# A fused attention, gelu-layer and expert kernel: its hand-written order made anew, with the second weight matrix narrowed in PSUM

## The chip, the cores and the metric

The kernel runs on one core of one Trainium2 chip. The metric is the device time of one launch in microseconds, and the time before is the median of three runs. The engines are TensorE (PE in the views, its weight loads PEld), VectorE (DVE), ScalarE (ACT), GpSimd (POOL) and SyncE (SP), which only issues transfers here. L931 is line 931 of the kernel.

## The reference

Three layers follow each other. First comes attention over 4 batches of 576 positions with 8 heads of 64, in which a position sees itself and the 63 before it; then a feed-forward layer with the gelu form h * sigmoid(1.702 h); then a layer of 8 experts of which each token takes its best two.

```python
scores = np.where(mask, (q @ k.T) / 8, -1e9)      # mask: 0 <= row - column < 64
x = softmax(scores) @ v                            # 2304 tokens x 512
h = x @ w_in                                       # 512 x 2048, float64
x = (h * (1.0 / (1.0 + np.exp(-1.702 * h)))) @ w_out   # 2048 x 512, float64
noisy = x @ w_gate + np.log1p(np.exp(x @ w_noise)) * noise
top2, top2_w = best_two(noisy)                     # weights: softmax of the two
out[t] = sum over the two of top2_w * (np.maximum(x[t] @ w1[e], 0.0) @ w2[e])
```

## The kernel before, in words

The 2304 tokens make 18 tiles of 128. A tile holds 128 rows of one batch; tiles 8 and 17 hold the last 64 rows of two batches each. Three tiles make a chunk (c = 0 to 5). A chunk's attention leaves xT, its first layer turns that into 16 products (f = 0 to 15) and its second layer sums these up into three output tiles. Every operand of a matmul is held as two float16 halves (a high part and the rest, "lo"), and a product is three matmuls (high by high, high by low, low by high). After the six chunks come the eight experts, in which rows are gathered by slot and the results are added into the output.

**The order written out.** For chunks 0 and 1, and the attention of tiles 0 to 9, every engine's order is the text SEQ, a list of some 760 short names; the loop behind `manual = tc.manual_schedule` emits them one after the other, and each engine works through its own in that order. A name's first part is a function (the table `ops`), its numbers are a tile, a piece or an f. The ones that matter here:

- `lk`, `lq`, `lv`: loads of a tile's k, q, v (lines 126 to 160), issued by SyncE. `wl`: load of one of 32 pieces of the two gelu-layer matrices (line 202), SyncE too.
- `na`, `nb`, `nc`: three VectorE steps (lines 214, 220, 226) that narrow a piece from float64, read as pairs of 32-bit words, to float32. Pieces 0 to 15 are of the first matrix, 16 to 31 of the second. `ch`, `cs`, `cl`: high half and scaling (ScalarE), low half (GpSimd, line 256).
- Tiles below NPE: `pt_` transposes q or k on TensorE (line 524), `ph_` and `pl_` take the halves out of PSUM (ScalarE 533, VectorE 537), `tp`, `th`, `tl` the same for the probabilities (600, 604, 607), and the scores are made by line 514. Other tiles: `qh` (ScalarE 401), `ql` (GpSimd 410), `kt` (SyncE 417), `q2` (two VectorE copies, 421 and 422), `qt` (SyncE 427), and for the probabilities `ph`, `pl`, `pt` (580, 583, 588), with the scores of line 488. `sh`, `sl`, `st` make tile 2's k once more in the second form for tile 3.
- `sc`, `mm`, `ex`, `rc`, `nm`, `pv`: scores, mask and maximum, exponentials, reciprocal, normalising, probability times V. `vh`, `vl`: halves of v. `e1`, `e2`: high and low half of xT (ScalarE 632, VectorE 638).
- `s1.f`, `t1.f`: the 12 matmuls of the first layer's product f of chunk 0 and 1 (line 667), into PSUM buffers "h" (two), for some f of chunk 0 "y" (two). `gt`, `gm`, `gh`, `gl` (and `ut` to `ul` for chunk 1): tanh (672), gelu product (675), high and low half (678, 681).
- `s2.f`, `z2`: second layer of chunk 0 and 1 (line 702). `yh`, `yl`: output halves (707, 710). `x2`, `lo`: SyncE transposes an output tile (739), TensorE makes its logits (750 to 753). `ra` to `ri`: routing.
- `cn`, `cg`, `cz`, `fd`: transfers of the noise (8), the gate weights (2), a zero row (1) and the slot table's fill (1), issued by SyncE (lines 345, 350, 355, 356, 339, 382).

**Behind the order.** The rest is placed by slots, one per 12 or so matmuls: the list `slots` holds the matmul steps from chunk 2 on, and before each slot all `tasks` that are due by it are emitted (`at`). Tile 10's loads and preparation are due between the slots 52 and 57 and so come right behind the order, tile 11's eight slots later. The steps of the routing of chunk c are due at fixed slots behind the chunk: `route_g` (three rank matmuls, line 825, that wait for r_M of line 814) at 12.

The buffers that the change touches are drawn from pools by tag: "r" (one PSUM bank), "h" (two PSUM banks), "wf" (two SBUF buffers of float32), "wst" (three SBUF buffers for loaded pieces). A new use of a tag waits until the use that many places earlier has been read.

Of the kernel before, what the change touches and what calls it, by code (L numbers as in the profile page):

```python
# [37 lines left out]
NPE = 3  # L38
# [7 lines left out]
pl_.2.1 wl.5 lv.2 rc.1.0 st.2 nc.3 cl.2 vl.1 na.4 tp.0.1 sc.2.0 lq.3 th.0.1 nm.1.0 mm.1.1 wl.6 lk.5 tp.1.0 tl.0.1 ch.3
nb.4 nc.4 cs.3 fc sc.2.1 va.1 ex.1.1 wl.7 th.1.0 na.5 rc.1.1 mm.2.0 nm.1.1 ch.4 vh.2 nb.5 tp.1.1 qh.3 mm.2.1 cl.3 nc.5
cs.4 pv.0.1 ql.3 ex.2.0 ex.2.1 wl.16 cl.4 na.6 nb.6 e1.0 rc.2.0 vl.2 nc.6 q2.3 ch.5 kt.3 ch.6 cs.5 wl.8 cl.5 e2.0
th.1.1 lq.5 tl.1.0 tl.1.1 va.2 cs.6 na.7 nb.7 cl.6 rc.2.1 nm.2.1 nm.2.0 pv.1.0 pv.1.1 qh.5 nc.7 na.16 nb.16 ch.7 na.8
nc.16 qt.3 tp.2.0 nb.8 e1.1 cs.7 e2.1 cl.7 th.2.0 tl.2.0 nc.8 tp.2.1 ch.16 cs.16 wl.9 th.2.1 lv.3 ch.8 sc.3.1 tl.2.1  # L50
pv.2.0 pv.2.1 sc.3.0 lk.4 na.9 cs.8 mm.3.1 e1.2 cl.8 wl.10 lq.4 e2.2 wl.11 nb.9 ex.3.1 cl.16 nc.9 s1.4 rc.3.1 s1.2
lv.4 ql.5 ch.9 na.10 s1.1 cs.9 nb.10 wl.18 gt.4 qh.4 nm.3.1 nc.10 ch.10 cl.9 cs.10 gm.4 gt.2 na.11 cl.10 nb.11 nc.11
gh.4 mm.3.0 s1.0 gt.1 ch.11 ql.4 vh.3 gm.2 cs.11 gh.2 gm.1 wl.12 gh.1 ex.3.0 s1.10 cl.11 ph.3.1 na.18 fd nb.18 gt.10
q2.4 kt.4 nc.18 gm.10 s1.7 ch.18 gh.10 na.12 gl.4 gt.0 s1.5 gl.2 wl.17 cs.18 rc.3.0 qt.4 s1.11 gm.0 nb.12 gt.5 na.17
wl.13 q2.5 pl.3.1 cl.18 pt.3.1 gm.5 gl.1 nc.12 nb.17 gt.11 gl.10 sc.4.0 gh.5 gm.11 nm.3.0 s1.8 s1.9 ch.12 nc.17 gt.7
# [24 lines left out]
e2.9 ri.0 yh.3 yl.3  # L80
# [17 lines left out]
def fused_kernel(ctx, tc, q, k, v, w_in, w_out, w_gate, w_noise, noise, w1, w2, out, cap=CAP):  # L98
# [186 lines left out]
    def consts_a():  # L285
# [11 lines left out]
        for t in range(3):  # L297
            dve.tensor_copy(m[0:64, t, 0:64], le[0:64])
            dve.tensor_copy(m[0:64, t, 64:128], gt[0:64])
            dve.tensor_copy(m[64:128, t, 0:64], (le if t == 2 else gt)[64:128])  # L300
            dve.tensor_copy(m[64:128, t, 64:128], (gt if t == 2 else le)[64:128])
# [169 lines left out]
    def scores(i, g):  # L471
# [562 lines left out]
    for c in range(NCH):  # L1034
# [7 lines left out]
        for fn, dt, dl in ((route_a, 5, 3.1), (route_b, 6, 3.2), (route_c, 7, 3.3), (route_d, 8, 3.4), (route_e, 10, 3.5),  # L1042
                           (route_f, 11, 3.6), (route_g, 12, 5), (route_h, 12, 5.2), (route_i, 13, 5.1)):
# [135 lines left out]
```

## Time and profile before

| what | us |
|---|---|
| three runs | 953.22, 956.4, 961.06 |
| median | 956.4 |
| the profiled execution | 955.65 |
| its span, first to last instruction | 954.0 |

The profile is one execution. Its rows give busy time, mean time of one instruction and the idle time of the engine just before a group, with what ended it ("releaser"). A row of the timeline gives start, length, engine, line, operation, and in brackets an idle time before it and its releaser. PEclk is the clock granted to TensorE as a share of full speed.

### The profile page before, as it was taken

What the parts mean: (1) busy time and instruction counts of PE and PEld (TensorE: products, weight loads), DVE (VectorE), ACT (ScalarE), POOL (GpSimd) and SP (SyncE); (2) the same over time, 40 slices, a digit from 0 to 9 for tenths busy, and PEclk for the clock granted to TensorE, in tenths of its full rate; (3) what the DMA queues carried; (4) which work ended last, traced back from release to release, by engine and by line L of the source; (5) the groups of instructions that cost most, each with busy time, mean ns of one, the idle gap of its engine ahead of it and who ended that gap; (6) DMA issues with size and microseconds to landing.
All of it is one profiled execution on the core that took longest, in us unless ns stands there. A gap on an engine that the chain in (4) does not pass through costs nothing. (4 is left out here: it accounts for less than half of the span.)

```text
span 954.0 us, 16355 instructions
## 1 busy us (share of the span) xinstructions
PE 883.7 (93%) x6315; PEld 504.0 (53%) x6315; DVE 501.3 (53%) x1020; ACT 388.5 (41%) x884; POOL 381.2 (40%) x372
## 2 busy tenths in 40 slices
PE   6597899997889999989999999998999999999994
PEld 4464445544545544644544556655564747465561
DVE  7999998762662662681372732354252525243220
ACT  5677576632552752751551421243140405141110
POOL 3467768523571561561361432341314132322111
PEclk9999999998899999999999999999999999999997
DMA  9999689936778737812137992798594949493212
GB/s 224 204 221 238 139 228 168 186 70 126 203 196 147 129 61 142 175 27 67 45 114 169 183 195 38 170 264 194 110 223 75 239 77 244 90 216 74 32 20 39
DMA packets 264948, 137.47 MB, mean 144 GB/s; under 512 B 217120, under 2 KB 241504, under 8 KB 264864
## 3 DMA queue, kind: packets, MB, share of 16 engines
q1 hardware_dynamic: 228640, 76.55, 41.3%
q0 software_dynamic: 11680, 27.30, 13.7%
q10 hardware_dynamic: 24544, 32.51, 11.8%
q8 instruction: 51, 0.84, 0.4%
q14 instruction: 33, 0.27, 0.1%
HBM read 76.46 MB, written 21.07 MB: 102 GB/s over the span
## 5 line engine op out<-in xcount | busy, mean ns | idle before, releaser
L931 PE MATMUL o<-w,gb 128*128 128x512 f16 x960 | 209.9, 379 | 0.6 <-DVE gb L914 0.6
L702 PE MATMUL y<-w,gb 128*128 128x512 f16 x816 | 186.8, 382 | 4.8 <-DVE gf L675 3.3
L924 PEld LDWEIGHTS <-w 128*128 128x128 f16 x1536 | 150.1, 98 | 63.2 <-issue 2.7
L667 PEld LDWEIGHTS <-w 128*128 128x128 f16 x1152 | 112.3, 100 | 95.9 <-issue 25.4
L954 POOL DMA_INDIRECT out_dram<-ot,me x40 | 70.3, 1758 | 231.3 <-DVE ot L951 227.2
L931 PEld LDWEIGHTS <-gb 128*128 128x128 f16 x960 | 93.6, 98 | 111.4 <-DVE gb L914 1.5
L667 PE MATMUL h<-xT,w 128*128 128x384 f16 x744 | 138.0, 339 | 14.6 <-DVE gf L675 12.0
L702 PEld LDWEIGHTS <-gb 128*128 128x128 f16 x864 | 82.6, 98 | 101.8 <-issue 9.2
L924 PE MATMUL h<-xe,w 128*128 128x384 f16 (+1 forms) x840 | 126.5, 302 | 2.4 <-DVE gb L914 2.4
L681 POOL TENSOR_TENSOR gb<-gf,gb 128x384 f16<-128x384 f32 x96 | 95.8, 1004 | 81.1 <-ACT gb L678 78.6
L951 DVE TENSOR_SCALAR ot<-o,me 128x512 f32<-128x512 f32 x40 | 30.0, 751 | 140.4 <-PE o L931 122.6
L267 DVE SCALAR_TENSOR_TENSOR w<-wst,w 128x1024 f16<-128x1024 f32 x64 | 79.4, 1241 | 45.5 <-ACT w L248 45.5
L924 PE MATMUL y<-xe,w 128*128 128x256 f16 (+1 forms) x696 | 102.1, 297 | 0.0
L913 ACT ACTIVATE gb<-y 128x256 f16<-128x256 f32 (+1 forms) x58 | 24.9, 430 | 179.5 <-PE y L924 179.4
L248 ACT ACTIVATE w<-wst 128x1024 f16<-128x1024 f32 x64 | 67.5, 1056 | 39.3 <-DVE w L267 14.2
L908 POOL DMA_INDIRECT xg<-x2buf,me x40 | 43.2, 1080 | 81.3 <-DMA me<-xmeta 40.3
L667 PE MATMUL y<-xT,w 128*128 128x384 f16 x408 | 71.5, 330 | 0.9 <-DVE gf L675 0.9
L678 ACT ACTIVATE gb<-gf 128x384 f16<-128x384 f32 x96 | 49.3, 516 | 40.6 <-DVE gf L675 39.8
L562 ACT ACTIVATE sm<-sm,st 128x128 f32<-128x128 f32 x144 | 55.9, 390 | 12.0 <-DVE st L556 11.9
L410 POOL TENSOR_TENSOR qk<-kq,qk 128x1024 f16<-128x1024 f32 x15 | 32.9, 2195 | 68.7 <-ACT qk L401 67.5
L913 ACT ACTIVATE gb<-h 128x384 f16<-128x384 f32 (+1 forms) x70 | 30.7, 439 | 63.3 <-PE h L924 62.3
L914 DVE SCALAR_TENSOR_TENSOR gb<-h,gb 128x384 f16<-128x384 f32 (+1 forms) x70 | 34.6, 494 | 40.1 <-ACT gb L913 40.1
(163 smaller groups left out, 962.7 us busy)
## 6 DMA issues: line engine op xcount, KB each, us to landing
wst<-in_moe_w_dram ACTq DMA_DIRECT2D x62, 512.0 KB, 4.4
wst<-in_moe_w_in_dram SPq DMA_DIRECT2D x16, 512.0 KB, 5.0
wst<-in_moe_w_out_dram SPq DMA_DIRECT2D x16, 512.0 KB, 4.0
x2buf<-R SPq DMA_DIRECT2D x18, 256.0 KB, 3.1
kq<-in_k_dram SPq DMA_DIRECT2D x16, 256.0 KB, 5.5
kq<-in_q_dram SPq DMA_DIRECT2D x16, 256.0 KB, 4.2
vv<-in_v_dram SPq DMA_DIRECT2D x16, 256.0 KB, 4.7
out_dram<-z POOLq DMA_DIRECT2D x3, 1280.0 KB, 5.8
```

The source lines that it names most:

```text
L248: act.activation(o[:, 0], i, AF.Copy, scale=s)
L267: dve.scalar_tensor_tensor(o[:, 1], i, s, o[:, 0], op0=ALU.mult, op1=ALU.subtract)
L562: act.activation(sm[:, u, :], sm[:, u, :], AF.Exp, bias=st[:, 0, u:u + 1], accum_out=st[:, 1, u:u + 1])
L667: pe.matmul(hp, w[:, a, d, fs], xt[:, x + d, :], start=n == 0, stop=n == 11)
L678: act.activation(g1[:, f, 0], GF[c, f], AF.Copy)
L681: pool.tensor_tensor(g1[:, f, 1], GF.pop((c, f)), g1[:, f, 0], op=ALU.subtract)
L702: pe.matmul(YP[i], g1[:, f, a, 128 * j:128 * j + 128], w[:, s, f % 8, :], start=f == 0 and a + s == 0, stop=f == 15 and a == 1)
L908: pool.indirect_dma_start(out=xg, out_offset=None, in_=src, in_offset=bass.IndirectOffsetOnAxis(ap=ME[e, part][:, t, 9:10], axis=0))
L913: act.activation(o[:, 0], hp, AF.Relu)
L924: pe.matmul(hp, w[:, a, d, 128 * f:128 * f + 128], x[:, s + d, :], start=m == 0, stop=m == 11)
L931: pe.matmul(yp, lhs[:, f, a, :], w[:, s, f, :], start=f == 0 and a + s == 0, stop=f == 7 and a == 1)
L954: s = pool.indirect_dma_start(out=out, out_offset=bass.IndirectOffsetOnAxis(ap=ids, axis=0), in_=ot, in_offset=None, compute_op=ALU.add)
```

## The change

What it does, in six parts:

- SEQ is written anew: the same operations in another sequence, apart from tile 3, which is handled as tiles 0 to 2 are (NPE 3 to 4), and tile 10, whose loads and preparation (`lk`, `lq`, `lv`, `qh`, `ql`, `kt`, `q2`, `qt`, `vh`, `vl`, `va`) now stand in the list.
- The second matrix's pieces: the first two narrowing steps write to a PSUM buffer of the tag "h" and the third reads it and writes to "wf", as the first matrix's pieces do with "r".
- `cn`, `cg`, `cz`, `fd` (12 transfers) are issued by GpSimd.
- Tiles 8 and 17 load v in two transfers of 128 rows instead of four of 64, with the older 64 rows in partitions 0 to 63; the mask and the score columns of these tiles are swapped to match.
- `route_g`, `route_h`, `route_i` and the scatters of chunks 1 to 4 are due one slot later.
- Behind the list nothing else differs; tasks that the list has done are left out.

```diff
-NPE = 3
+NPE = 4
...
 SEQ = """
-lk.0 cid lq.0 pt_.0.0 wl.0 lk.1 ph_.0.0 pt_.0.1 lq.1 ca pl_.0.0 ph_.0.1 fa pl_.0.1 na.0 sc.0.0 pt_.1.0 ph_.1.0 sc.0.1
...
+cid lk.0 wl.0 lq.0 pt_.0.0 fa pt_.0.1 ca na.0 ph_.0.0 ph_.0.1 nb.0 pl_.0.0 nc.0 pl_.0.1 ch.0 wl.2 sc.0.0 na.2 nb.2
...
+z2.2.0 nm.8.0 pt.7.1 ul.14 yl.2 lv.9 sc.9.0 cn ex.8.1
+ph.8.0 pv.7.0 rc.8.1 lo.0 pv.7.1 e1.7 um.10 uh.12 nm.8.1 uh.10 pl.8.0 t1.13 vh.9 vl.9 ul.12 x2.1 ut.13 x2.2 z2.1.1
+ph.8.1 mm.9.0 pl.8.1 mm.9.1 vl.8 e2.7 ex.9.0 ex.9.1 ul.10 ci t1.15 pt.8.0 um.13 uh.13 ql.10 lo.1 z2.2.1 rc.9.0 pv.8.0
...
 """
...
-        sp.dma_start(vv[0:64], rows(v, b, 512, 64))
-        sp.dma_start(vv[64:128], rows(v, b, 448, 64))
-        sp.dma_start(vb[0:64], rows(v, b + 1, 512, 64))
-        sp.dma_start(vb[64:128], rows(v, b + 1, 448, 64))
+        sp.dma_start(vv, rows(v, b, 448, 128))
+        sp.dma_start(vb, rows(v, b + 1, 448, 128))
...
-            o = NW[key, p] = T(pm, [128, 512], F32, "r", 1) if key[0] == "in" else T(mp, [128, 512], F32, "wf", 2)
+            o = NW[key, p] = T(pm, [128, 512], F32, *(("r", 1) if key[0] == "in" else ("h", 2)))
...
-            o = T(mp, [128, 512], F32, "wf", 2) if key[0] == "in" else i
+            o = T(mp, [128, 512], F32, "wf", 2)
...
-        sp.dma_start(x2buf[0], C["z"])
+        pool.dma_start(x2buf[0], C["z"])
...
-            sp.dma_start(nz[:, i0:i0 + 4], noise[b * S:b * S + 512].rearrange("(t p) e -> p t e", p=128))
+            pool.dma_start(nz[:, i0:i0 + 4], noise[b * S:b * S + 512].rearrange("(t p) e -> p t e", p=128))
...
-                       (route_f, 11, 3.6), (route_g, 12, 5), (route_h, 12, 5.2), (route_i, 13, 5.1)):
+                       (route_f, 11, 3.6), (route_g, 13, 5), (route_h, 13, 5.2), (route_i, 14, 5.1)):
```

Counted in the two lists, VectorE's operations up to and with `e2.5` (tile 5's low half of xT, for which the first matmul of `t1` waits):

| operation | old | new |
|---|---|---|
| narrowed pieces of the first matrix | 16 | 16 |
| narrowed pieces of the second matrix | 8 | 10 |
| `pl_` and `tl` (low halves taken out of PSUM) | 12 | 16 |
| `q2` (swaps) | 4 | 3 |
| `mm`, `rc`, `gm`, `vl`, `e2` | 13, 12, 16, 6, 6 | 13, 12, 16, 6, 6 |

And TensorE's from the first `t1` to the end of the list, in both: 16 `t1`, 9 `s2`, 12 `z2`, 6 `sc`, 8 `pv`, 3 `lo`. Between the first `s1` and the first `t1` the new list has two `tp` more. Ahead of the first `s1` it has two `pt_` more and otherwise the same counts.

## Rows read from the trace of the kernel before

**Rows 1.** Timeline of TensorE: first s1, first t1, end of the written order.

```profile
53.84 3.02 PE L667 MATMUL h<-xT,w 128*128 128x384 f16 x12
...
122.57 5.85 PE L667 MATMUL h<-xT,w 128*128 128x384 f16 x35 [0.45 <-DVE xT L638]
...
219.34 4.06 PE L667 MATMUL h<-xT,w 128*128 128x384 f16 x24
```

**Rows 2.** Busy time by stretch: length, engines (x instructions), clock, transfer share, GB/s.

```profile
0.00:53.80 53.80, 35.36 (x384) 27.49 (x384) 46.93 (x99) 34.62 (x93) 21.64 (x26) 1.00 0.96 220
53.80:121.80 68.00, 57.20 (x494) 31.55 (x488) 64.67 (x93) 46.33 (x120) 52.05 (x44) 0.95 0.86 200
121.80:185.20 63.40, 57.65 (x497) 32.34 (x496) 53.62 (x82) 40.02 (x109) 44.01 (x56) 0.97 0.96 189
185.20:219.30 34.10, 34.10 (x250) 16.08 (x244) 21.46 (x75) 14.71 (x38) 8.11 (x7) 1.00 0.39 77
219.30:280.00 60.70, 50.52 (x401) 28.09 (x400) 33.18 (x90) 29.86 (x77) 37.00 (x36) 0.89 0.77 193
```

**Rows 3.** TensorE's waits, 53.8 to 219.4: total us, times, longest.

```profile
PE h L667 <- DVE gf L675: 3.6, 3, 2.2
PE x L623 <- DVE xT L638: 3.4, 1, 3.4
```

**Rows 4.** VectorE's groups by shape, 0 to 219: busy us, mean ns, idle before.

```profile
L226 DVE SCALAR_TENSOR_TENSOR wf<-wst,wf 128x512 int32<-128x512 int32 x16 | 18.7, 1167 | 0.2
L220 DVE SCALAR_TENSOR_TENSOR wf<-wst,wf 128x512 int32<-128x512 int32 x16 | 16.1, 1006 | 0.2
L214 DVE TENSOR_SCALAR wf<-wst 128x512 int32<-128x512 int32 x16 | 14.7, 921 | 3.0 <-POOL w L256 3.0
...
L220 DVE SCALAR_TENSOR_TENSOR r<-wst,r 128x512 int32<-128x512 int32 x16 | 11.0, 689 | 0.2
L214 DVE TENSOR_SCALAR r<-wst 128x512 int32<-128x512 int32 x16 | 11.0, 686 | 0.1
L226 DVE SCALAR_TENSOR_TENSOR wf<-wst,r 128x512 int32<-128x512 int32 x16 | 10.9, 680 | 0.8
...
L421 DVE COPY qk<-qk 128x512 f16<-128x512 f16 x7 | 8.5, 1219 | 0.0
...
L422 DVE COPY qk<-qk 128x512 f16<-128x512 f16 x7 | 4.6, 658 | 0.0
```

**Rows 5.** Timeline of TensorE: scores in both forms, one group of transposes.

```profile
21.28 2.38 PE L514 MATMUL s<-kT,qT 64*128 64x64 f16 x36
...
28.38 1.11 PE L600 MATMUL y<-idn,sm 128*128 128x128 f32 x4
...
147.15 0.77 PE L488 MATMUL s<-kT,qT 128*128 128x64 f16 x24
```

**Rows 6.** Timelines behind the order: SyncE, ScalarE, GpSimd, VectorE, TensorE.

```profile
222.83 0.43 SPq L128 DMA_DIRECT2D kq<-in_k_dram  x1
...
227.71 1.06 ACT L401 ACTIVATE qk<-kq 128x1024 f16<-128x1024 f32 x1 [7.57 <-DMA kq<-in_q_dram]
...
228.84 2.12 POOL L410 TENSOR_TENSOR qk<-kq,qk 128x1024 f16<-128x1024 f32 x1 [29.14 <-ACT qk L401]
...
231.00 0.29 DVE L421 COPY qk<-qk 128x512 f16<-128x512 f16 x1 [10.13 <-POOL qk L410]
...
229.52 0.19 PE L753 MATMUL r<-wr,x2T 128*128 128x32 f16 x1 [1.21 <-DMA x2T<-R]
...
232.01 3.22 PE L667 MATMUL h<-xT,w 128*128 128x384 f16 x13 [2.12 <-DVE gf L675]
...
236.38 0.24 PE L488 MATMUL s<-kT,qT 128*128 128x64 f16 x1 [1.15 <-DMA qT<-qk]
```

**Rows 7.** TensorE's waits, 219 to 500: total us, times, longest.

```profile
PE r L825 <- DVE r_M L814: 3.3, 2, 2.6
```

**Rows 8.** GpSimd's own transfer issues (ns min/median/max), and a VectorE copy beside them.

```profile
L202 POOL DMA_DIRECT2D wst<-in_moe_w_dram x2: 826/899/972, 165.1 to 168.9; - x2
...
165.43 3.73 DVE L421 COPY qk<-qk 128x512 f16<-128x512 f16 x1
```

More of the change, by code (lines that the diff above doesn't have):

```diff
@@ L46 @@
[L46 to L55, printed above, removed]
@@ new lines @@
+pv.1.0 pt_.3.0 vh.2 ex.2.0 fd lk.4 na.6 vh.3 mm.2.1 th.1.1 ch.5 wl.7 tl.1.1 rc.2.0 pt_.3.1 ph_.3.0 cl.4 na.17 ex.2.1
+nm.2.0 nb.6 pl_.3.0 pv.1.1 vl.2 ph_.3.1 e1.1 lq.4 va.2 tp.2.0 rc.2.1 pl_.3.1 nc.6 cs.5 nm.2.1 tp.2.1 th.2.0 ch.6 cs.6
+cl.5 nb.17 th.2.1 tl.2.0 na.7 nc.17 lk.5 tl.2.1 qh.4 cl.6 e2.1 ch.17 wl.8 sc.3.1 nb.7 pv.2.0 pv.2.1 vl.3 nc.7 cs.17
+ql.4 e1.2 mm.3.1 na.8 lq.5 e2.2 nb.8 wl.16 sc.3.0 wl.9 qh.5 q2.4 s1.1 lk.6 cl.17 ch.7 nc.8 na.16 ex.3.1 kt.4 rc.3.1
+cs.7 ch.8 ql.5 s1.2 wl.10 cs.8 na.9 qt.4 cl.7 cl.8 nb.16 nb.9 nc.9 gt.2 nc.16 gt.1 ch.9 gm.1 ch.16 mm.3.0 wl.11 gm.2
@@ new lines @@
+cs.16 s1.6 cs.9 gt.6 s1.0 gh.1 nm.3.1 na.10 lq.6 gt.0 wl.12 cl.9 nb.10 tp.3.1 s1.9 gl.1 gh.2 gm.0 ex.3.0 gm.6 nc.10
+th.3.1 gl.2 cl.16 q2.5 wl.13 gt.9 rc.3.0 na.11 va.3 gm.9 nb.11 gh.0 gl.0 ch.10 s1.5 sc.4.0 cs.10 gt.5 nc.11 gm.5 ch.11
+sc.4.1 nm.3.0 gh.6 cs.11 cl.11 tp.3.0 tl.3.1 s1.8 gh.9 na.12 qh.6 mm.4.0 s1.3 mm.4.1 nb.12 cl.10 ex.4.0 qt.5 nc.12
+gl.6 th.3.0 ql.6 na.13 gt.8 gt.3 wl.18 ch.12 gm.3 tl.3.0 s1.4 gl.9 gh.5 s1.10 cs.12 gm.8 pv.3.0 gh.3 rc.4.0 nb.13
+wl.14 nc.13 gl.5 na.18 nm.4.0 cl.12 ex.4.1 gh.8 gl.8 s1.7 gl.3 rc.4.1 gt.10 kt.5 ch.13 na.14 wl.20 nb.18 nm.4.1 kt.6
@@ new lines @@
+gm.10 lv.4 nc.18 gt.4 gt.7 cs.13 gm.4 q2.6 wl.15 sc.5.0 ph.4.0 ch.18 gm.7 ph.4.1 qt.6 cl.13 s1.11 gh.10 na.20 pl.4.0
+nb.14 nb.20 cs.18 pl.4.1 gh.7 nc.14 ch.14 mm.5.0 pv.3.1 cs.14 cl.18 ex.5.0 nc.20 sc.5.1 wl.19 cl.14 gt.11 ch.20 na.15
+s1.12 nb.15 wl.24 nc.15 gh.4 s1.14 ch.15 gm.11 s2.0 vh.4 gl.10 gl.4 e1.3 s2.1 gt.12 rc.5.0 sc.6.1 gh.11 nm.5.0 gt.14
+cs.20 lv.5 mm.5.1 pt.4.0 gm.12 wl.22 vl.4 cs.15 na.19 ex.5.1 nb.19 cl.20 vh.5 nc.19 gh.12 gl.7 ch.19 sc.6.0 cs.19
+gm.14 rc.5.1 e2.3 cl.15 na.24 ph.5.0 nb.24 nc.24 s1.15 gt.15 gh.14 s2.2 wl.21 ch.24 pt.4.1 pv.4.0 gm.15 vl.5 na.22
@@ new lines @@
+cl.19 na.21 cs.24 nb.22 gl.11 nc.22 pl.5.0 wl.28 nm.5.1 s2.3 nb.21 ch.22 cl.24 ph.5.1 va.5 pv.4.1 cs.22 pl.5.1 e1.4
+pt.5.0 nc.21 mm.6.1 ch.21 cl.22 s1.13 na.28 s2.4 e2.4 pv.5.0 wl.23 cs.21 gh.15 gt.13 cl.21 nb.28 s2.5 gm.13 gh.13
+nc.28 gl.14 na.23 nb.23 ch.28 cs.28 pt.5.1 pv.5.1 e1.5 ex.6.1 nc.23 gl.15 cl.28 wl.25 e2.5 ch.23 na.25 nb.25 nc.25
+cs.23 s2.6 t1.0 wl.26 lk.7 rc.6.1 gl.12 ut.0 um.0 t1.2 cl.23 lq.7 lv.6 ut.2 mm.6.0 uh.0 ex.6.0 t1.3 um.2 lk.9 ut.3
+lq.9 wl.27 na.26 um.3 nb.26 nc.26 gl.13 nm.6.1 s2.7 qh.7 ch.25 ch.26 ph.6.1 ql.7 pl.6.1 ul.0 cs.26 t1.4 t1.6 s2.8 vh.6
@@ L81 @@
+pt.8.1 z2.2.2 nm.9.0 ul.13 ph.9.0 ut.15 z2.1.2 rc.9.1 um.15 kt.10 uh.15 nm.9.1 pl.9.0 pv.8.1 lv.10 ph.9.1 ul.15 z2.1.3
+lo.2 z2.2.3 yh.4 pl.9.1 ra.0 cu rb.0 pt.9.1 yl.4 rq.0 pt.9.0 e1.8 rd.0 e2.8 vh.10 z2.0.0 re.0 yh.5 q2.10 qt.10 pv.9.0
+rf.0 z2.0.1 pv.9.1 z2.0.2 e1.9 rh.0 e2.9 rg.0 vl.10 z2.0.3 yh.3 va.10 yl.5 ri.0 yl.3
 """
@@ L297, in consts_a @@
         for t in range(3):
[L298 to L301, printed above, removed]
+            dve.tensor_copy(m[0:64, t, 0:64], (gt if t == 2 else le)[0:64])
+            dve.tensor_copy(m[0:64, t, 64:128], (le if t == 2 else gt)[0:64])
+            dve.tensor_copy(m[64:128, t, 0:64], gt[64:128])
+            dve.tensor_copy(m[64:128, t, 64:128], le[64:128])
         dve.memset(m[0:64, 1, 64:128], MASK)
@@ L349, in consts_n @@
                     r0 = (b + j) * S + 512
-                    sp.dma_start(nz[64 * j:64 * j + 64, i], noise[r0:r0 + 64])
+                    pool.dma_start(nz[64 * j:64 * j + 64, i], noise[r0:r0 + 64])
         C["nz"] = nz
@@ L354, in consts_g @@
         wg = T(cst, [128, 4, 2 * E], F32, "wg")
-        sp.dma_start(wg[:, :, 0:E], w_gate.rearrange("(c p) e -> p c e", p=128))
-        sp.dma_start(wg[:, :, E:], w_noise.rearrange("(c p) e -> p c e", p=128))
+        pool.dma_start(wg[:, :, 0:E], w_gate.rearrange("(c p) e -> p c e", p=128))
+        pool.dma_start(wg[:, :, E:], w_noise.rearrange("(c p) e -> p c e", p=128))
         C["wg"] = wg
@@ L481, in scores @@
             parts = [[(64 * j, 64 * j + 64, c0, c0 + 64, kk, 64 * j) for j in range(2)]
-                     for c0, kk in ((0, k1), (64, KT[i]))]
+                     for c0, kk in ((0, KT[i]), (64, k1))]
         for pp in parts:
@@ L1048, in fused_kernel @@
             for a in range(2):
-                at(t0 + (5.4 if last else (14 if c else 17 + P["r0"]) + 2 * j + a), scatter, c, j, a)
+                at(t0 + (5.4 if last else (15 if c else 17 + P["r0"]) + 2 * j + a), scatter, c, j, a)
     for n in range(4):
```

43 lines of the change are left out of this document (14 added, 29 removed).

## The prediction, made before the changed kernel ran

> **What bounds the kernel now.** I read the stretches first, because the change is confined to the order written out by hand and the few steps behind it. The order ends where TensorE starts on the third chunk, at 219.34 us [rows 1]. Up to 121.8 us the limit is VectorE: it works 46.93 of the first 53.80 us and 64.67 of the next 68.00, while TensorE stands still for 18.44 and 10.80 us [rows 2]. From 121.8 to 185.2 us VectorE still works 53.62 of 63.40, TensorE idles 5.75, and from 185.2 us to the end of the order TensorE never stops. Then, from 219.3 to 280 us, TensorE loses 10.18 us again, with a granted clock of 0.89 [rows 2]. In the view of TensorE's waits the two largest after the first first-layer matmul are on VectorE: 3.6 us on the gelu product (gf) and 3.4 on the low half of xT [rows 3]. So work taken from VectorE moves TensorE up to about 185 us; work given to TensorE costs nothing only while it idles.
>
> **VectorE, the narrowing of the second matrix.** The three narrowing steps of one piece take 0.921 + 1.006 + 1.167 = 3.094 us with the intermediate in SBUF (second matrix) and 0.686 + 0.689 + 0.680 = 2.055 with it in PSUM (first matrix), over 16 pieces each [rows 4]. The edit gives the second matrix the PSUM form: 16 x 1.04 = 16.6 us less VectorE work. That the same integer steps would not get faster in PSUM is excluded by these rows.
>
> **Part A, up to the first matmul of chunk 1's first layer.** At 122.57 us this matmul waited for tile 5's xT low half on VectorE [rows 1], so VectorE's work ahead of that step sets it. By the counts listed with the change, both orders have the same masks, maxima, gelu products and v splits ahead of it. The old one has 8 pieces of the second matrix, the new one 10; the new one has 4 more low-half subtractions (tile 3 on TensorE) and one q swap less. So 10 x 2.055 - 8 x 3.094 = -4.2 us; the four subtractions read PSUM as the narrowing's last step does, at about 0.68 us [rows 4], +2.7; the swap's two copies, 1.219 + 0.658 [rows 4], -1.9. Sum -3.4 us: the first t1 comes at about 119.2 us. VectorE also idles 53.80 - 46.93 + 68.00 - 64.67 = 10.2 us there; the new order may shrink or stretch this. I take no change; the ends are a gain of 10.2 and, as nothing excludes it, a loss as large.
>
> **Tile 3 on TensorE.** Two score groups of 36 matmuls (2.38 us) take the place of 24 (0.77), and four groups of transposes at 1.11 us are added [rows 5]: 3.2 + 4.4 us. The probability-times-V groups keep 24 matmuls each, in the slower form, which by the scores' ratio (2.38/36 against 0.77/24) doubles each of them; estimate 0.8 each, 1.6 us. Together 9.3 us, all before the first t1, where TensorE idles 29.2 us: cost 0. Only two transposes and the two V groups (3.8 us) stand behind the first first-layer matmul, where 10.80 us idle remain as cover; uncovered they would cost 3.8. GpSimd, ScalarE and the transposing transfers lose work by it; I count nothing for that.
>
> **Part B, from the first t1 to the end of the order.** Both orders hold the same TensorE work there (the counts agree), and it took 219.34 - 122.57 = 96.8 us. Losses in it: 5.75 us idle, and a clock of 0.97 over 63.4 us [rows 2], which as a mix of its two levels, 2.4 and 1.2 GHz, is 3.8 us at half speed, 1.9 us lost: 7.65 in all. VectorE has 6 pieces of 2.055 left where it had 8 of 3.094, 12.3 instead of 24.8 us; tile 10 brings back one swap (1.9) and one v split, whose price no row here has (no more than another 2). It falls from 53.6 to about 45 of 63 us. The waits on VectorE should go; waits on a transfer stay, and the borrowed PSUM buffers (below) can make new ones. I take 5 of the 7.65; the ends are 7.65 and the cost of the second rival. Then the order ends at 119.2 + 91.8 = 211.0 instead of 219.3: 8.4 us gained by A and B.
>
> **Part C, tile 10's loads.** At present SyncE issues them only at 222.83, behind the transpose of the last output rows. From there runs one chain: ScalarE waits 7.57 us for the q load and begins at 227.71, GpSimd begins its difference at 228.84, VectorE's copy stands 10.13 us at the head of its queue until 231.00, and the gelu product of the new chunk, queued behind, makes TensorE wait 2.12 us; the scores wait 1.15 for qT, and the second logits transpose, which SyncE issues behind these loads, makes it wait 1.21 [rows 6]. All of it is moved into the order: 4.5 us of stalls. What is late next is tile 11, whose preparation is not moved. Ends: all 10.18 us idle and the lost half of the clock, (1 - 0.89) x 2 x 60.7 / 2 = 6.7 [rows 2], against 0 if tile 11 stalls in its place. I take 4.5.
>
> **Part D, the rank matmuls one slot later.** TensorE waited for r_M in two places, 3.3 us in all [rows 7]. A slot is some 2 us of matmuls, so most of it is hidden; I take 1.5, between 0 and 3.3, and a loss of the same size if the later rank step delays the scatters behind it.
>
> **Issues.** Twelve transfers go from SyncE to GpSimd: the fill of the slot table, the zero row, eight for the noise, two for the gate weights. One issue holds GpSimd for 0.826 to 0.972 us [rows 8], so 12 x 0.9 = 10.8 us, of which the eight for the noise, 7.2, come in one piece. Queued behind those are low halves of g1 that TensorE reads only after 24 first-layer and 24 second-layer matmuls; at the 5.85 us that 35 first-layer ones took [rows 1] that is 8 us or more of cover. I take 0; uncovered it costs 7.2. SyncE loses these and two loads at tile 8; nothing waits there now that I price. On the sign of their conflict with VectorE the row says that VectorE loses: a copy, 1.219 us on average [rows 4], lasted 3.73 while GpSimd worked and issued [rows 8]. The Trainium skill, "SBUF - State Buffer", section "SBUF: two separate sides", says that a transfer issued from GpSimd is starved while VectorE runs an operation in a two-port mode, with 3.1 us in place of 0.62; by that, twelve would cost GpSimd some 37 us (an estimate from that page), and no row here shows an issue so long.
>
> **Sum.** 8.4 + 4.5 + 1.5 = 14.4 us. The profiled execution took 955.65 us (span 954.0); 955.65 - 14.4 = 941.25. It lies 0.75 under the median of the runs, so I predict 942 us.
>
> **Rivals.**
> 1. *VectorE's time turns into waiting.* In a fixed order each step also waits for ScalarE, GpSimd and the transfers. Then A and B give nothing, tile 3's 3.8 us are uncovered, C and D stay: 955.65 + 0.75 + 3.8 - 6 = 954.2 us. For it: the transfer engines are 0.86 to 0.96 busy up to 185 us [rows 2]. Against: the largest waits name VectorE. Chance 0.28.
> 2. *The borrowed buffers, slower than before.* The second matrix's intermediate now takes one of the two "h" buffers in which first-layer results land. Each of 16 pieces leaves TensorE a single one until its third step is through. A wait for such a buffer shows now as h <- gf, 1.2 us on average, 2.2 at most [rows 3]. Sixteen at 1.2 add 19 us: 961; at 2.2, 35 us: 977. It decides from 12 waits at the mean or 7 at the longest, where the 14.4 are eaten. Against: VectorE runs ahead of TensorE in the new order and the three steps last 2.1 us. Chance 0.14.
> 3. *Starved issues.* If each noise issue lasts as long as that copy, 8 x 3.73 = 30 us stand in front of the low halves; with 8 us of matmuls as cover, 22 are lost: 964 us. Chance 0.04.
> 4. *More than forecast.* If VectorE's idle time (10.2), all of B's 7.65 and C's 16.9 went, the gain would be 3.4 + 10.2 + 7.65 + 16.9 + 3.3 = 41 us. Halfway between forecast and that, 929 us. Chance 0.10.
>
> **How the numbers follow.** My forecast has 0.44, its own range 936 to 948. About 1%, 9.6 us, is what a measurement can tell from no change. Faster takes the fourth rival and nearly all of the forecast, and a little of the first: 0.56. Same takes most of the first and the mild end of the second: 0.31. Slower is the rest, the second at more than 1.5 us a piece, and the third: 0.13. The range 930 to 961 leaves out most of the fourth rival below and the worse parts of the second and third above.
>
> **What would show it.** Right: the narrowing steps of the second matrix at 0.68 to 0.70 us; first t1 near 119, third chunk near 211; no ScalarE wait on tile 10's q load. Wrong: waits of h on a narrowing step (rival 2); first t1 at 122 or later with VectorE idle more than 10 us before it (rival 1); low halves of g1 late behind GpSimd's issues (rival 3); a new stall of 2 us or more at tile 11 that takes back part C.

## The result, and the profile after

| | before | after |
|---|---|---|
| runs beside each other | 952.13 to 961.06 (4) | 930.49 to 938.58 (4) |
| median, us | 954.81 | 932.1 |
| the profiled execution | 955.65 | 933.35 |
| its span | 954.0 | 931.6 |

The ratio is 0.9752, 95% interval 0.971 to 0.9793: some 22 us faster. The forecast was 942, its range 930 to 961.

Line numbers after the helpers have moved by two (L667 is now L665, L675 is L673, L702 is L700); in runs whose list was edited they are four higher than that (L669 for L665, and so on). First the marks, from the timeline of TensorE of the changed kernel: first s1, first t1, first matmul of the third chunk, as in [rows 1].

```profile
48.49 0.98 PE L665 MATMUL h<-xT,w 128*128 128x384 f16 x2
...
110.68 6.01 PE L665 MATMUL h<-xT,w 128*128 128x384 f16 x36
...
208.09 4.06 PE L665 MATMUL h<-xT,w 128*128 128x384 f16 x24
```

The three come 5.4, 11.9 and 11.3 us earlier than before (one of the 36 matmuls of the first t1 had run at 121.80 there; the mark at 122.57 is where the other 35 went on), and the fourth chunk starts at 283.59 where it started at 305.60. Cut at these four marks, the windows tell in which stretch the time went. The columns are those of [rows 2]. The kernel before:

```profile
0.00:53.84 53.84, 35.40 (x384) 27.49 (x385) 46.97 (x99) 34.66 (x93) 21.68 (x26) 1.00 0.96 220
53.84:122.57 68.73, 57.48 (x492) 31.65 (x489) 65.40 (x95) 47.06 (x123) 52.78 (x44) 0.95 0.86 202
122.57:219.34 96.77, 91.47 (x739) 48.32 (x739) 74.30 (x154) 53.96 (x142) 51.35 (x63) 0.98 0.76 148
219.34:305.60 86.26, 76.08 (x597) 40.40 (x595) 39.26 (x103) 35.84 (x94) 44.06 (x40) 0.92 0.75 176
```

And the changed kernel, between its own marks:

```profile
0.00:48.49 48.49, 34.89 (x416) 26.91 (x417) 44.87 (x97) 33.67 (x90) 20.28 (x25) 0.89 0.91 227
48.49:110.68 62.19, 57.47 (x498) 32.90 (x496) 60.27 (x105) 49.18 (x132) 47.29 (x44) 0.95 1.00 222
110.68:208.09 97.41, 90.93 (x741) 48.30 (x740) 67.52 (x151) 53.13 (x138) 52.82 (x74) 0.98 0.84 160
208.09:283.59 75.50, 71.82 (x597) 39.03 (x596) 37.68 (x100) 35.01 (x92) 40.98 (x39) 0.98 0.75 177
```

The lengths change by -5.35, -6.54, +0.64 and -10.76 us; what is left of the two spans, -0.4, falls behind the fourth chunk (it holds a loss of 2.7 us at the very end of the kernel, which experiment 8 shows). So all the gain lies in two places, ahead of the first t1 and directly behind the written order. The stretch between them, in which VectorE lost 6.8 us of work (74.30 to 67.52), became no shorter.

The narrowing steps of the second matrix fell as forecast. VectorE's groups by shape, up to 208 us, which answer to [rows 4]:

```profile
L218 DVE SCALAR_TENSOR_TENSOR h<-wst,h 128x512 int32<-128x512 int32 x16 | 11.0, 689 | 0.2
...
L224 DVE SCALAR_TENSOR_TENSOR wf<-wst,h 128x512 int32<-128x512 int32 x16 | 11.0, 685 | 2.4 <-POOL w L254 1.5
...
L212 DVE TENSOR_SCALAR h<-wst 128x512 int32<-128x512 int32 x16 | 10.9, 684 | 0.1
```

What TensorE still waits for, from the start to 280 us (total us, times, longest), beside [rows 3]:

```profile
PE h L665 <- DVE gf L673: 6.8, 3, 3.9
PE y L598 <- POOL sm L570: 6.0, 4, 3.3
...
PE h L665 <- DVE wf L224: 2.6, 2, 2.3
PE x L621 <- DMA PT<-p: 1.8, 1, 1.8
```

The third line shown is the price of the borrowed buffers, a wait of h on the third narrowing step: 2.6 us in all, two times, and not sixteen. The longest wait of the first line is new. It shows in three timelines of the changed kernel, here VectorE, GpSimd and TensorE:

```profile
139.92 4.59 DVE L452 SCALAR_TENSOR_TENSOR v<-vv,v 128x512 f16<-128x512 f32 x1
144.43 0.68 DVE L552 SCALAR_TENSOR_TENSOR sm<-s,msk 128x512 f32<-128x512 f32 x1
145.15 0.69 DVE L554 TENSOR_REDUCE st<-sm 128x4 f32<-128x512 f32 x1
145.75 0.54 DVE L673 SCALAR_TENSOR_TENSOR gf<-gf,h 128x384 f32<-128x384 f32 x1
```

```profile
139.23 2.14 POOL L408 TENSOR_TENSOR qk<-kq,qk 128x1024 f16<-128x1024 f32 x1
141.32 2.63 POOL L679 TENSOR_TENSOR gb<-gf,gb 128x384 f16<-128x384 f32 x3
```

```profile
146.34 3.55 PE L665 MATMUL h<-xT,w 128*128 128x384 f16 x12 [3.90 <-DVE gf L673]
```

VectorE's split of v (vl.7) has both inputs in SBUF. It is over only half a microsecond behind the third of GpSimd's products, 4.59 us where this line's median is 0.688. The gelu product of 0.54 us stands in the queue behind it (with a mask step and a maximum between), and TensorE waits 3.90 us for that product.

Behind the order, ScalarE no longer waits for tile 10's q, and TensorE has these waits from 208.1 to 300 us, beside [rows 6]:

```profile
PE h L665 <- DVE gf L673: 2.1, 1, 2.1
PE r L824 <- DVE r_mc L816: 0.8, 1, 0.8
PE r L751 <- DMA x2T<-R: 0.7, 1, 0.7
```

### The profile page after: what moved, and what is told of

Its sections match the earlier page's. It is cut to its first block, busy times and chain, and to the rows that moved or that the text cites. A ratio compares the mean times of both kernels' runs of the same rounds, so it can differ in the third digit from the quotient of the medians.

```text
span 931.6 us, 16441 instructions
## 1 busy us (share of the span) xinstructions
PE 878.2 (94%) x6355; PEld 502.9 (54%) x6355; DVE 483.9 (52%) x1022; ACT 388.2 (42%) x884; POOL 372.0 (40%) x380
## 5 line engine op out<-in xcount | busy, mean ns | idle before, releaser
L700 PE MATMUL y<-w,gb 128*128 128x512 f16 x816 | 185.1, 380 | 0.0
L665 PEld LDWEIGHTS <-w 128*128 128x128 f16 x1152 | 111.5, 99 | 94.1 <-issue 23.1
L665 PE MATMUL h<-xT,w 128*128 128x384 f16 x744 | 137.4, 338 | 14.7 <-DVE gf L673 12.1
L700 PEld LDWEIGHTS <-gb 128*128 128x128 f16 x864 | 82.3, 98 | 94.9 <-issue 1.2
L679 POOL TENSOR_TENSOR gb<-gf,gb 128x384 f16<-128x384 f32 x96 | 91.1, 954 | 81.5 <-ACT gb L676 81.3
L665 PE MATMUL y<-xT,w 128*128 128x384 f16 x408 | 70.0, 326 | 1.5 <-DVE gf L673 1.5
L877 POOL DMA_INDIRECT xmeta<-rm,slot x36 | 38.5, 1070 | 39.9 <-DVE ov L865 31.5
```

Of the source, the lines that this page charges most:

```text
L665: pe.matmul(hp, w[:, a, d, fs], xt[:, x + d, :], start=n == 0, stop=n == 11)
L679: pool.tensor_tensor(g1[:, f, 1], GF.pop((c, f)), g1[:, f, 0], op=ALU.subtract)
L700: pe.matmul(YP[i], g1[:, f, a, 128 * j:128 * j + 128], w[:, s, f % 8, :], start=f == 0 and a + s == 0, stop=f == 15 and a == 1)
```

## The experiments

Each run is given by its median and its ratio to the kernel before on the same chip, with the 95% interval. "The order's end" is the first matmul of the third chunk.

**The changed kernel again, as a mark.**

> The changed kernel as it is, as the mark for the runs beside it: 0.975 of the kernel before, first t1 at 110.7 us, third chunk at 208.1, about 932 us. All theories expect the same.

934.49 us, ratio 0.9793 (0.976 to 0.9826), the order's end at 208.81, the fourth chunk at 282.55. The marks repeat within 1 us.

**1. The second matrix's intermediate back in SBUF, all else as changed.**

```diff
-            o = NW[key, p] = T(pm, [128, 512], F32, *(("r", 1) if key[0] == "in" else ("h", 2)))
+            o = NW[key, p] = T(pm, [128, 512], F32, "r", 1) if key[0] == "in" else T(mp, [128, 512], F32, "wf", 2)
...
-            o = T(mp, [128, 512], F32, "wf", 2)
+            o = T(mp, [128, 512], F32, "wf", 2) if key[0] == "in" else i
```

> The new order with the second matrix narrowed through SBUF again. Theory (VectorE's own time sets the first 110 us): ten pieces dearer by 1.0 to 1.2 us ahead of the first t1, six behind it, so first t1 8 to 12 us later than 110.7, third chunk 8 to 14 us later than 208.1, total 940 to 946 us. Rival (the new sequence alone gives the gain, VectorE has room): first t1 and third chunk within 3 us, total up to 935. Second rival (the borrowed h buffers cost about what the faster steps give): no change or up to 3 us faster.

951.74 us, ratio 0.9966 (0.9945 to 0.9988): 17 us of the gain go with this edit, more than the theory had. The first t1 comes at 125.14 (111.70 in the mark), and the order's end lies at 226.76, later than in the old order; both are beyond the theory's ranges. VectorE's groups of this run, up to 222 us, show two losses:

```profile
L212 DVE TENSOR_SCALAR wf<-wst 128x512 int32<-128x512 int32 x16 | 17.3, 1084 | 8.8 <-POOL w L254 8.8
L224 DVE SCALAR_TENSOR_TENSOR wf<-wst,wf 128x512 int32<-128x512 int32 x16 | 14.9, 932 | 0.3
L218 DVE SCALAR_TENSOR_TENSOR wf<-wst,wf 128x512 int32<-128x512 int32 x16 | 14.9, 931 | 0.2
```

The steps take 47.1 us where they take 32.9 in the changed kernel, 14.2 more. And VectorE now stands 8.8 us at the first step for a wf buffer: with the intermediate in SBUF, one of the two wf buffers is held from the first step on and not only from the third. Next experiment.

**2. The same with three wf buffers** (the room is taken from the output tiles "R", three instead of four).

```diff
-            o = NW[key, p] = T(pm, [128, 512], F32, *(("r", 1) if key[0] == "in" else ("h", 2)))
+            o = NW[key, p] = T(pm, [128, 512], F32, "r", 1) if key[0] == "in" else T(mp, [128, 512], F32, "wf", 3)
...
-            o = T(mp, [128, 512], F32, "wf", 2)
+            o = T(mp, [128, 512], F32, "wf", 3) if key[0] == "in" else i
...
-        RT[i] = T(mp, [128, 2 * DM], F16, "R", 4)
+        RT[i] = T(mp, [128, 2 * DM], F16, "R", 3)
```

> The run with the second matrix narrowed through SBUF (951.7 us) once more, with three buffers of float32 pieces instead of two (and three of output rows instead of four, for the room). There VectorE waited 8.8 us for such a buffer, which is taken from the first narrowing step on and not from the third. Theory (the steps' own length costs the 17 us): 948 to 952. Rival (the early hold of the buffers costs about half of it): VectorE's wait for GpSimd nearly gone and 5 to 9 us less, 943 to 947.

949.87 us, ratio 0.9915 (0.9886 to 0.9944). The same groups:

```profile
L218 DVE SCALAR_TENSOR_TENSOR wf<-wst,wf 128x512 int32<-128x512 int32 x16 | 24.7, 1544 | 0.2
L224 DVE SCALAR_TENSOR_TENSOR wf<-wst,wf 128x512 int32<-128x512 int32 x16 | 17.5, 1091 | 0.3
L212 DVE TENSOR_SCALAR wf<-wst 128x512 int32<-128x512 int32 x16 | 12.5, 787 | 0.0
```

The 8.8 us are gone and the order's end comes at 221.73, 5.0 us earlier than in experiment 1 and 12.9 later than in the mark. The steps themselves take longer still, 54.7 us. So of the 18 us at the order's end some 5 go with the early hold of the buffer, and some 13 remain with the longer steps; that one output tile fewer costs nothing was not tried by itself. The time is within the theory's 948 to 952; the medians of experiments 1 and 2 differ by only 1.9 us, and the profiled execution is the fastest of the nine (944.82 us).

**3. Tile 10 out of the list** (its eleven names removed; their steps are then placed by the slots behind the order, as before).

```diff
-... qt.8 uh.8 lk.10 um.14 ph.7.0 uh.14 nm.7.1 s2.15 yh.2 yh.0 lq.10 pl.7.0 ...
+... qt.8 uh.8 um.14 ph.7.0 uh.14 nm.7.1 s2.15 yh.2 yh.0 pl.7.0 ...
```

> The new order without tile 10's eleven steps, which are then placed by the slots as before. Theory (the whole gain behind the order, 10.8 us between the third and the fourth chunk's start, is tile 10's chain): that stretch goes from 75.5 back to about 86 us, total 941 to 944. Rival (the gain there comes from the later rank step and from SyncE's shorter queue): the stretch grows by at most 5 us, total 933 to 937. The order itself may end 0 to 2 us earlier, since VectorE and GpSimd have less to do in it.

943.45 us, ratio 0.9868 (0.9837 to 0.99): 9 us come back. The order's end is nearly unchanged (209.50 against 208.81), and the stretch to the fourth chunk is 83.4 us instead of 73.7. Among TensorE's waits there are 3.6 us for qT, in three places; two of these in its timeline are tile 11's:

```profile
242.22 0.20 PE L490 MATMUL s<-kT,qT 128*128 128x64 f16 x1 [1.33 <-DMA qT<-qk]
243.45 1.12 PE L490 MATMUL s<-kT,qT 128*128 128x64 f16 x23 [1.03 <-DMA qT<-qk]
```

In the kernel before, tile 11 had waited 1.23 and 1.12 us for qT at 252.64 and 253.97. I had not counted these, for only tile 10's preparation is moved.

**4. The old order, with tile 10 put into it and nothing else.**

```diff
-... qt.9 ... ex.8.1 ... pl.8.1 ... pt.8.1 ... e2.8 ... pt.9.0 ... rf.0 ... rh.0 ...
+... qt.9 lk.10 lq.10 ... ex.8.1 qh.10 ... pl.8.1 ql.10 ... pt.8.1 kt.10 lv.10 ... e2.8 q2.10 ... pt.9.0 qt.10 ... rf.0 vh.10 ... rh.0 vl.10 va.10 ...
```

> The old kernel with nothing but tile 10's loads and preparation put into its list, where its tiles 8 and 9 are prepared and behind. Theory (that chain is independent of the rest): the stretch between the third and fourth chunk's start goes from 86.3 to about 76 us, the order ends 0 to 2 us later, total 945 to 949. Rival (it needs the new order's room on VectorE): the order ends as much later as is gained behind it, total 952 to 957.

945.11 us, ratio 0.9859 (0.9809 to 0.9908). The order's end stays at 219.17. The window from there to the fourth chunk, beside the last line of the kernel before's table above:

```profile
219.17:293.89 74.72, 70.19 (x597) 38.29 (x596) 37.06 (x100) 35.03 (x92) 41.38 (x39) 1.00 0.75 179
```

It is 11.5 us shorter than before (86.26 to 74.72). TensorE's idle time fell from 10.18 to 4.53 us, 5.65 less. The same matmuls also ran at a clock of 1.00 instead of 0.92, and were busy for 70.19 instead of 76.08 us, 5.89 less. In the new order the same comparison, experiment 3 against the first mark, shows 6.33 us more idle time (9.94 against 3.61) and matmuls busy for 3.34 us more (73.47 against 70.13) at a clock of 0.96 instead of 1.00. So both halves go with the edit in either order; the half that is the clock differs more, 3.3 and 5.9 us in single executions. By the medians this part of the change is worth 9 us in the new order and 12 in the old one, and needs no other part.

**5. The routing steps due early again** (chunks 1 to 4 a slot earlier, as before).

```diff
-                       (route_f, 11, 3.6), (route_g, 13, 5), (route_h, 13, 5.2), (route_i, 14, 5.1)):
+                       (route_f, 11, 3.6), (route_g, 12, 5), (route_h, 12, 5.2), (route_i, 13, 5.1)):
...
-            at(t0 + (5.4 if last else (15 if c else 17 + P["r0"]) + 2 * j + a), scatter, c, j, a)
+            at(t0 + (5.4 if last else (14 if c else 17 + P["r0"]) + 2 * j + a), scatter, c, j, a)
```

> The new kernel with the routing steps and scatters at their earlier slots. Theory: waits on r_M come back in two places, 1 to 3.3 us, total 933 to 935.5; the stretch between the third and fourth chunk's start stays at 75.5. Rival (the later rank step carries part of the gain behind the order): 5 us or more, total 937 and up.

936.28 us, ratio 0.9804 (0.9775 to 0.9833), 1.8 us over the mark and not resolved from it. The wait itself is plain, in TensorE's waits from 209 to 500 us of this run and then, from 208.8 us, of the mark:

```profile
PE r L823 <- DVE r_M L812: 5.3, 3, 2.6
```

```profile
PE r L823 <- DVE r_M L812: 1.4, 2, 0.8
```

3.9 us of this wait are saved, but the waits on gelu products and on x2T in the same stretch are larger in the mark (7.5 + 2.7 against 4.1 + 1.2 + 0.6, 4.3 us). So in these two executions all of it is given back by what is late next, and no gain of the later slots is shown.

**6. The twelve transfers issued by SyncE again.**

```diff
-        pool.dma_start(x2buf[0], C["z"])
+        sp.dma_start(x2buf[0], C["z"])
...
-            pool.dma_start(nz[:, i0:i0 + 4], noise[b * S:b * S + 512].rearrange("(t p) e -> p t e", p=128))
+            sp.dma_start(nz[:, i0:i0 + 4], noise[b * S:b * S + 512].rearrange("(t p) e -> p t e", p=128))
```

(and the same for the other noise rows, the two gate weights and the slot table's fill)

> The new kernel with its twelve transfers issued by SyncE again. Theory: nothing waits for either queue, so within 2 us of the changed kernel's 934.5. Rival (starved issues): GpSimd's own issues delay low halves or VectorE's copies, so this one is 3 us or more faster. The other side: SyncE's queue is what the change relieved, so this one is 3 us or more slower.

931.18 us, ratio 0.9717 (0.9669 to 0.9765). The marks up to the fourth chunk agree with the first mark run within 0.4 us, and the interval just touches that run's. By itself this left open whether the issues cost anything; experiments 8 and 9 come back to it.

**7. Tile 7's v split moved behind a later gelu product** (vl.7 and va.7 behind um.9).

```diff
-... va.6 ul.11 vl.7 ut.9 va.7 mm.7.0 t1.5 um.9 t1.8 ...
+... va.6 ul.11 ut.9 mm.7.0 t1.5 um.9 vl.7 va.7 t1.8 ...
```

> The new kernel with one move in the list: tile 7's v split (and the copies that wait for it) behind the gelu product of f = 9, no more ahead of it. In the changed kernel that split, two inputs in SBUF, lasted 4.59 us from 139.92 while GpSimd worked through 139.2 to 144.0, and TensorE waited 3.9 us for the gelu product behind it. Theory: the stall goes, the order ends 3 to 5 us earlier, total 929 to 932. Rival (another step of VectorE is caught by the same run of GpSimd, or TensorE waits next for the transfer behind the split): under 1 us gained.

934.1 us, ratio 0.9754 (0.9714 to 0.9794), the order's end at 207.28, 1.5 us before the first mark's and not the theory's 3 to 5. The 3.90 us are gone and another wait stands in their place, on the transpose of tile 6's probabilities; TensorE's timeline of this run:

```profile
150.23 0.28 PE L625 MATMUL x<-PT,va 128*64 128x64 f16 x6 [2.85 <-DMA PT<-p]
```

SyncE's own queue tells why. Its lines L465 and L466 are the copies of `va`. The first pair is va.6; the second is va.7, which must wait for the v split just moved, and the transpose pt.6.0 is queued behind it:

```profile
140.64 0.58 SPq L465 DMA_DIRECT2D va<-v  x1
141.27 0.61 SPq L466 DMA_DIRECT2D va<-v  x1
145.61 0.46 SPq L465 DMA_DIRECT2D va<-v  x1
146.12 0.60 SPq L466 DMA_DIRECT2D va<-v  x1
146.82 1.29 SPq L590 DMA_TRANSPOSE PT<-p  x1
```

From 141.88 to 145.61 SyncE issued nothing.

**8. Three moves, on one chip with a second mark, and then with SyncE's issues too.** The second mark, the changed kernel again:

> The changed kernel again, as a mark for the two runs beside it. All theories: 931 to 935 us, end of the order near 208 to 209 us.

936.81 us, ratio 0.9798 (0.9762 to 0.9835); the order's end at 209.13. The three moves: vl.7 as in experiment 7, va.7 behind pt.6.0, and the third narrowing step of piece 20 ahead of a mask step.

```diff
-... na.20 pl.4.0 nb.14 nb.20 cs.18 pl.4.1 gh.7 nc.14 ch.14 mm.5.0 pv.3.1 cs.14 cl.18 ex.5.0 nc.20 ...
+... na.20 pl.4.0 nb.14 nb.20 nc.20 cs.18 pl.4.1 gh.7 nc.14 ch.14 mm.5.0 pv.3.1 cs.14 cl.18 ex.5.0 ...
...
-... va.6 ul.11 vl.7 ut.9 va.7 mm.7.0 t1.5 um.9 t1.8 cs.30 q2.9 ex.7.0 ul.1 s2.12 pt.6.0 ...
+... va.6 ul.11 ut.9 mm.7.0 t1.5 um.9 vl.7 t1.8 cs.30 q2.9 ex.7.0 ul.1 s2.12 pt.6.0 va.7 ...
```

> Three names of the list moved: v's low half of tile 7 behind um.9, its transposed-side copy va.7 behind pt.6.0 (so that SyncE's queue is not held), and the third narrowing step of piece 20 ahead of chunk 1's mask step. Theory (a step at the head of an in-order queue is what stops TensorE, and its place alone decides): the 3.9 us wait on the gelu product at 146 us and the 2.3 us wait on the narrowing step at 85 us both go, no wait on a probability transpose takes their place, the order ends 3 to 6 us earlier (203 to 205 us) and the time is 927 to 931 us. Rival (the stretch is full, so that each removed wait comes back at the next step, as in the run that moved the two v steps alone): waits of the same sum stand at other places, the order ends at 207 us or later, time 932 to 935 us.

933.11 us, ratio 0.9773 (0.9738 to 0.9809). The order's end is at 204.69, 4.4 us before the second mark's and within the theory's 203 to 205. TensorE's timeline shows both spots, first the 2.32 us wait of the changed kernel at 85.45, then the 3.90:

```profile
86.14 0.50 PE L669 MATMUL h<-xT,w 128*128 128x384 f16 x2 [1.86 <-ACT w L250]
88.10 3.17 PE L669 MATMUL h<-xT,w 128*128 128x384 f16 x10 [1.46 <-POOL w L258]
...
149.13 0.28 PE L625 MATMUL x<-PT,va 128*64 128x64 f16 x6 [0.80 <-DMA PT<-p]
```

At the second spot 0.80 is left: there the theory holds, and the queue of SyncE was what experiment 7 had missed. At the first spot nothing is won; the matmul then waits for its weights, on ScalarE and GpSimd, 3.3 us together. The time itself is not resolved from the second mark, and lies where the rival had it (932 to 935) and not at the theory's 927 to 931.

With SyncE's twelve issues on top (the edit of experiment 6):

> The same three moves, and the twelve transfers issued by SyncE again. If the issues cost GpSimd's neighbours nothing (theory): within 1.5 us of the run with the moves alone. If GpSimd's issues delay the low halves behind them (rival): 2 to 4 us less than that run. If SyncE's queue is what is full: 2 to 4 us more.

926.36 us, ratio 0.9697 (0.9667 to 0.9726), six runs from 925.02 to 929.19, below all six of the moves alone (929.95 to 937.72) and clear of the second mark's interval. The theory, that the issues cost nothing, falls. The rival's mechanism is not seen either, since the order's end (205.14) and the fourth chunk (279.01, against 278.49 for the moves alone) are not earlier. The two profiled executions part behind that: from the fourth chunk to the last instruction the moves alone take 650.3 us and the version with SyncE's issues 645.5. More than half of these 4.8 us stand at the very end. GpSimd's last scatter, and the draining of its queue after that (the line's shortest, median and longest of three), for the moves alone:

```profile
914.26 1.55 POOL L956 DMA_INDIRECT out_dram<-ot,me  x1 [3.59 <-DVEq L975]
...
L1177 POOLq DRAIN  x3: 50/109/5420, 922.6 to 928.6; - x3
```

and with SyncE's issues:

```profile
912.61 1.55 POOL L956 DMA_INDIRECT out_dram<-ot,me  x1 [3.59 <-DVEq L975]
...
L1177 POOLq DRAIN  x3: 50/109/3419, 920.3 to 924.2; - x3
```

From the end of the scatter to the end of the span it is 12.99 us in the one and 10.34 in the other, 2.65 less, of which 2.00 are the longest drain. Every trace of this case agrees: 12.85 to 13.10 us and a drain of 5.42 in the nine that issue the twelve from GpSimd, 10.15 to 10.37 us and a drain of 3.42 in the five that issue them from SyncE, the kernel before among them. So the place of the twelve issues costs some 2.7 us at the end of the kernel. The remaining 2.2 us lie between the fourth chunk and the last scatter, a stretch that in the two marks, one and the same kernel, already differs by 3.2 us. Parts of it ran at another clock (0.91 for the moves alone and 1.00 with SyncE's issues, both from 380 to 400 and from 480 to 500 us).

**9. That kernel once more, on another chip.**

> The kernel with the three moves and SyncE's issues once more, in new runs. In the runs before, it and the kernel with the moves alone had the same marks up to the fourth chunk (279.0 and 278.5 us), and the difference stood behind them, in stretches with a clock of 0.91. If the place of the issues brings the higher mean clock: ratio to the kernel before near 0.970, mean clock of the span 0.984 to 0.987. If it was the draw of those runs: ratio 0.975 to 0.978, mean clock 0.978 to 0.982. The marks stay: end of the order near 205 us in either case.

927.56 us, ratio 0.9705 (0.9673 to 0.9737), mean clock of the six runs 0.984, the order's end at 204.94. The gain repeats. This version, three moves and SyncE's issues, beats both kernels: 26 to 28 us under the kernel before, and on the chip that ran both, 10 under the changed one. A higher mean clock goes with it in the six runs (0.984 again, against 0.980 for the moves alone), but is not needed for it: the profiled execution here had 0.980, about that of the moves alone (0.979), and its span is still 2.7 us shorter (926.1 against 928.8), with 10.37 us behind its last scatter. The three runs of this version at a clock of 0.980 took 926.42 to 927.98 us, no longer than the others (925.02 to 929.19). What makes up the rest of the 5.5 to 6.8 us between the medians stays open, and so does why GpSimd's drain at the end depends on transfers that landed long before.

## Why the prediction was right or wrong

The sign and the range were right and the size was short: 14.4 us forecast, 22.3 in the profiled executions. The terms fit worse than the sum: A and C were too small, B and the issues too favourable, and the errors partly cancelled, so that the range held owes something to luck.

- **Part A (forecast -3.4, measured -11.9): two steps mis-sized.** "I take no change" for VectorE's 10.2 idle microseconds was the larger of the two errors. VectorE worked 112.37 us before its mark and 105.14 of 110.68 after, so its idle time fell to 5.5: 4.7 us. The work fell by 7.2, not 3.4. In the old order the eight pieces of the second matrix cost 26.7 us ahead of that mark (9 first steps at 801 ns, 8 at 1225 and 8 at 1216), where the mean over the whole order gave 24.8; in the new order the ten pieces cost 21.1, where 20.6 were reckoned. The swaps lost 2.1 us (1.9 reckoned), the v splits 1.1 (nothing reckoned), and the low halves took 2.8 more (2.7 reckoned). The bound was rightly named for the old order. In the new one tile 5's low half was over at 110.16 and the first t1 began at 110.68 behind TensorE's own matmuls, without a wait, so the bound had moved.
- **VectorE's narrowing (1.04 us a piece): right, and worth more than its own time in this order.** The steps measure 684, 689 and 685 ns. Taking this edit back costs 17 us, part of it by a buffer hold that the prediction had not seen. The new sequence relies on it: without it the order ends 7.4 us later than the old one. That the edit alone would do as much in the old sequence was not tried.
- **Part B (forecast -5, measured +0.6): the step that failed.** "The waits on VectorE should go": they did not, they moved. In TensorE's waits behind the first t1 the new order has 4.7 us on gelu products (2.9 in the old one), 3.90 of it behind the late v split, and 1.8 on a probability transpose; TensorE's idle time there rose from 5.3 to 6.5 us. Experiment 8 shows that another place for two names turns 3.90 us into 0.80 here.
- **Part C (forecast -4.5, measured -10.8): mechanism right, size off.** The term left out tile 11's two waits for qT, which went too. It also left out the clock, which the prediction had worked out as an end of the range (6.7 us) and then set to nothing. Experiment 4 measures 5.65 us of idle and 5.89 us of slower matmuls.
- **Part D (forecast -1.5): not shown.** Its waits lie behind the fourth chunk. From there to the last scatter the changed kernel is 3.1 us shorter than the kernel before, no more than the two marks differ there (3.2). The waits on r_M fell, but by experiment 5 others took their place; the 1.8 us between its median and the mark's are not resolved from nothing.
- **Issues (forecast 0): wrong by some 2.7 us, at a place the prediction did not look at.** Rival 3 did not come. GpSimd's issues in the changed kernel take 0.5 to 1.0 us each; its groups by line, mean ns behind the busy time:

```profile
L343 POOL DMA_DIRECT2D nz<-in_moe_noise_dram x4 | 3.0, 752 | 0.0
L348 POOL DMA_DIRECT2D nz<-in_moe_noise_dram x4 | 2.1, 533 | 0.0
...
L380 POOL DMA_DIRECT2D xmeta<-gf x1 | 1.0, 966 | 0.0
```

  The price stands at the end of the kernel, where GpSimd's queue takes 2.7 us longer to come to rest (13.08 us behind the last scatter in the changed kernel, 10.34 in the kernel before). The runs that issue from SyncE are faster by 3.3 us by the medians of experiment 6 and the first mark (two chips), and by 6.75 by experiment 8 (one chip); what they have beyond the 2.7 is not shown to come from the issues. The Trainium skill, "SBUF — State Buffer", section "SBUF: two separate sides", advises to issue from SyncE or ScalarE because issues from GpSimd can be starved: the sign agrees, but these issues show no such wait.
- **Tile 3 (forecast 0): not contradicted.** The first two stretches shrank although TensorE took it on. It was not tried alone, nor were the v loads of tiles 8 and 17.
- **Rivals.** Rival 1 is what happened in part B alone. Rival 2 is 2.6 us, two waits. Rival 4 named idle time and clock as where more could come from, and most of it came from there.

## What to carry to other kernels

Where an engine sets the end of a stretch, count its idle time in that stretch as part of what shorter steps can win, and look which of its steps wait for buffers that others hold. A written order and the step lengths that it was made for belong together: the PSUM edit was worth 17 us in the new order and was not tried in the old one, while tile 10's loads were worth 9 to 12 in both. Before moving a name, list what its transfers hold up in the queue that issues them. And read a kernel's last 15 us too: which engine issued early transfers showed there, 2.7 us of it, and in no wait along the way.

## What the runs showed of the hardware

- A VectorE step with two SBUF inputs waited for more than the GpSimd operation that ran when it started. The v split of 4.59 us began during a GpSimd difference that ended at 141.37, and ended 0.56 us after the last of the three products that followed (143.95). In experiment 8 the same step began at 144.14, took 2.28 us, and again ended 0.55 us after GpSimd's third product. The Trainium skill, "SBUF — State Buffer", section "SBUF: two separate sides", has the shared ports held for one whole instruction of the engine that came first; if the split's turn had come right after the difference, it would have started at 141.37 and been over 0.68 us later. The trace has 144.51.
- A narrowing step over 128x512 took 787 to 1544 ns on average with its intermediate in SBUF, by step and kernel, and 680 to 692 ns in every kernel with its intermediate in PSUM.
- GpSimd's longest drain at the end of the program took 3.42 us in all five traces of kernels that issue the twelve early transfers from SyncE, and 5.42 us in all nine of kernels that issue them from GpSimd.
- The granted clock in the first stretch was 1.00 before and 0.89 after, with TensorE idle for less time in the second (13.6 against 18.4 us). A shorter idle time did not mean more clock.
